# Chunks of 2, 4, 4, 3, 3, 3, 2 units with shared sigmoid phases, 8 KB output rows and 64-row combine products in a fused RG-LRU and soft-MoE kernel

## The chip, the cores and the metric

The kernel runs on one core of one Trainium2 chip. The metric is the device time of one execution in microseconds (us). A core has five engines, each with its own instruction queue in program order: TensorE (PE), VectorE (DVE), ScalarE (ACT), GpSimd (POOL) and SyncE (SP), which here only issues DMAs. Matrix products go to PSUM, everything else lives in SBUF.

## The reference

The first half is a gated linear recurrence over 4 sequences of 5056 tokens with 256 channels, the second a soft mixture of experts over the resulting 20224 tokens.

```python
log_a = 8 * sigmoid(r_gate) * log(clip(sigmoid(a_param)))
a_t = exp(log_a);  norm = sqrt(max(1 - a_t*a_t, 1e-6))
x_gated = norm * sigmoid(i_gate) * x
h = a_t[:, t]*h + x_gated[:, t];  y[:, t] = h         # for t in range(S)
logits = y @ phi                                       # 32 slots = 8 experts x 4
slot_input = softmax_over_tokens(logits).T @ y
slot_out[e] = relu(slot_input[e] @ w1[e]) @ w2[e]      # w1 256x1024, w2 1024x256
out = softmax_over_slots(logits) @ slot_out
```

The slots need every token before the experts can run, and every output row needs the experts. So all of y is computed and reduced first, and the output is written at the end. Only the logits (20224 x 32) are kept.

## The kernel before, in words

Tokens are taken in 40 quads q of 512 (four blocks of 128; the last has 256). Units p hold two quads, but the first and the last hold one: 21 units. A planner adds tasks with names, durations and buffers, and `run_fixed` emits them in the order that is written out by hand in `ORDER`, a list for each engine (line 79). Durations only settle which buffer slot a task gets. SBUF has 20 big buffers `b` of 8 KB a partition (N_B, line 52).

For each quad, D tasks load r, i and x (tokens in rows of four, 4 KB a partition). TR (line 788) transposes r to channels on partitions, SR (799) takes tanh. EX (866) takes the exponential, for two units of a chunk together where a chunk has a pair (`second`, line 762), SQ (850) squares on POOL, RT (881) takes the root. SI (812, 814) takes the input gate's sigmoid, or tanh in units marked P or E in `IV`, U (834) multiplies with x on POOL, TU (900) transposes. ST (917) and the scan SC (934) run on DVE. The tokens of a unit stand along the free dimension of A, so that y is in A after SC. TY (958) transposes y back and YC (972, 974) copies it to `yn`.

ACT holds one set of functions at a time: tanh and exp, tanh and sigmoid, or sqrt. Units are grouped in chunks (`CHUNKS`, line 23), and ACT goes through a chunk in phases: SR and EX, then SI, then RT.

For every four quads there is a group g: LG (1009) makes the logits with four quads side by side in the 128 columns of PE, LE (1022) copies them and keeps a running maximum M, LD, TE (1053) and ES (1063) make the exponentials, AC (1083) sums them times y, AE (1099) adds into `accS` with the factor DM (1070). The last four quads are split: group 9 has two, group 10 has three segments of 256 tokens. The merge (MT, MX, MR, MC, WJ, WE, W, SP, SL, DN, RD) joins the four row sets; L1 (1331) and L2 (1379) are the experts, whose weights w1 and w2 are loaded behind the gates.

SO (1398) scales the slot outputs, RS (1401) spreads them over four row sets, SH and BD (1403 to 1412) split them in a high and a low part, in a block-diagonal form for two blocks of tokens. For each group, CT (1438) transposes the logits, CM, CS, CE, RR and CN make the softmax, CH and CL split it, HP (1503) transposes, HE (1514, 1516) copies, OT (1526) multiplies two blocks at once with 128 rows by 512 columns, OE (1538, 1540) copies to an output buffer, OD (1550) writes 4 KB a partition, 512 KB in all.

## Time and profile before

| | |
|---|---|
| median of 3 runs | 300.62 us (299.88 to 300.74) |
| profiled execution | 300.04 us, span 298.3 us |
| ACT_TABLE_LOAD | 26 of 1283 ns |
| moved | 100.02 MB, of which 20.71 MB written |

A row of a list of groups reads: line, engine, operation, output<-input, count, then busy us and mean ns, then the idle time ahead of it and what ended it. A row of the timeline reads: start us, busy us, engine, line, operation, count. A row of stretches gives the busy us of each engine between two times.

### The profile page before, as it was taken

How to read it: one execution, taken by the hardware profiler on the slowest of the kernel's cores; microseconds unless marked ns; L12 is line 12 of the kernel's file. 1: busy time of each engine (PE TensorE's matmuls, PEld its weight loads, DVE VectorE, ACT ScalarE, POOL GpSimd, SP SyncE). 2: the span in 40 equal slices, each digit the busy share in tenths (PEclk: the TensorE clock that was granted, in tenths of full speed). 3: DMA queues.
4: the chain of work that ended last, by engine and by line, in shares of the span. 5: the costliest groups of instructions: out<-in, count | busy, mean ns of one | idle time of the engine just before them, and what ended most of it. 6: DMA issues, size and time to landing. Idle time of an engine off the chain costs nothing.

```text
span 298.3 us, 5854 instructions
## 1 busy us (share of the span) xinstructions
PE 259.9 (87%) x2223; PEld 198.9 (67%) x2223; DVE 232.3 (78%) x289; ACT 251.2 (84%) x271; POOL 204.5 (69%) x150
## 2 busy tenths in 40 slices
...
GB/s 229 414 409 409 402 408 410 407 408 281 322 291 208 396 415 407 274 401 116 396 392 264 174 335 365 229 385 362 358 405 351 6 78 398 404 402 404 402 409 288
DMA packets 30287, 100.02 MB, mean 335 GB/s; under 512 B 3378, under 2 KB 3380, under 8 KB 30260
## 3 DMA queue, kind: packets, MB, share of 16 engines
...
q8 instruction: 17, 0.28, 0.4%
q14 instruction: 10, 0.08, 0.1%
...
HBM read 78.94 MB, written 20.71 MB: 334 GB/s over the span
## 4 chain that ended last, share of the span: by engine, by line
PE 35%; ACT 24%; DVE 14%; DMA 11%; POOL 6%; issue 6%; SPq 0%; ACTq 0%; POOLq 0%; DVEq 0%
DVE b L934 7%; PE bank L1526 7%; DMA b<-in_i_gate_dram 6%; PE pair L788 5%; ACT b L881 4%; DVE pair L917 4%; PE pair L900 4%; POOL b L834 4%; ACT b L812 3%; DMA st<-in_moe_w_dram 3%; ACT b L799 3%; ACT b L866 3%; PE one L1526 3%; ACT L881 3%; POOL b L850 2%
## 5 line engine op out<-in xcount | busy, mean ns | idle before, releaser
L850 POOL TENSOR_TENSOR b<-b 128x1024 f32<-128x1024 f32 (+2 forms) x41 | 73.6, 1816 | 9.0 <-ACT b L866 4.7
L834 POOL TENSOR_TENSOR b<-b,b 128x1024 f32<-128x1024 f32 x32 | 75.4, 2379 | 6.0 <-ACT b L814 4.3
L917 DVE SCALAR_TENSOR_TENSOR pair<-b,pair 128x1024 f32<-128x1024 f32 (+2 forms) x42 | 47.9, 1154 | 11.9 <-ACT b L881 8.1
L900 PE MATMUL pair<-ident,b 128*128 128x128 f32 x380 | 49.4, 278 | 7.3 <-DVE b L934 3.0
L900 PEld LDWEIGHTS pair<-ident,b 128*128 128x128 f32 x380 | 42.3, 143 | 15.7 <-POOL b L834 4.7
L934 DVE TENSOR_TENSOR_SCAN b<-b,pair 128x1024 f32<-128x1024 f32 (+6 forms) x26 | 47.6, 1848 | 0.2
L788 PE MATMUL pair<-ident,st 128*128 128x128 f32 x316 | 42.1, 280 | 5.2 <-DVE b L934 2.1
L934 DVE TENSOR_TENSOR_SCAN b<-b,b,pair 128x1024 f32<-128x1024 f32 (+2 forms) x22 | 45.4, 2073 | 0.4
L788 PEld LDWEIGHTS pair<-ident,st 128*128 128x128 f32 x316 | 35.4, 143 | 12.8 <-ACT b L799 4.9
L799 ACT ACTIVATE b<-pair 128x1024 f32<-128x1024 f32 (+1 forms) x40 | 39.4, 1012 | 4.6 <-PE pair L788 4.4
L866 ACT ACTIVATE b<-b,ca 128x2048 f32<-128x2048 f32 (+3 forms) x24 | 42.7, 1795 | 0.2
L958 PE MATMUL one<-ident,b 128*128 128x128 f32 x208 | 31.6, 281 | 7.2 <-DVE yn L974 2.5
L958 PEld LDWEIGHTS one<-ident,b 128*128 128x128 f32 x208 | 22.6, 141 | 17.3 <-DVE yn L974 6.6
L1526 PE MATMUL bank<-bd,hT 128*128 128x512 f32 x118 | 31.7, 400 | 0.3 <-DVE hT L1516 0.3
L1469 POOL TENSOR_TENSOR b<-b,rs_all 128x512 f32<-128x512 f32 (+2 forms) x11 | 10.6, 960 | 29.8 <-DVE rs_all L1461 23.2
L881 ACT ACTIVATE b<-b 128x2048 f32<-128x2048 f32 (+2 forms) x17 | 29.8, 1785 | 0.1
L1514 ACT CAST hT<-bank 128x512 fp32r<-128x512 f32 x14 | 8.3, 600 | 21.4 <-PE bank L1503 20.6
L812 ACT ACTIVATE b<-b 128x2048 f32<-128x2048 f32 x14 | 26.0, 1906 | 0.1
L1526 PEld LDWEIGHTS bank<-bd,hT 128*128 128x128 f32 x118 | 21.3, 188 | 5.4 <-ACT st L1538 0.8
L1538 ACT COPY st<-bank 128x512 f32<-128x512 f32 x33 | 18.8, 603 | 6.9 <-PE bank L1526 4.5
L974 DVE COPY yn<-one 128x512 f32<-128x512 f32 x32 | 21.2, 682 | 2.2 <-PE one L958 2.1
L1009 PE MATMUL one<-b,phi_sb 128*32 128x512 f32 x152 | 21.3, 618 | 0.0
...
## 6 DMA issues: line engine op xcount, KB each, us to landing
b<-in_x_dram SPq DMA_DIRECT2D x39, 512.0 KB, 7.4
st<-in_r_gate_dram SPq DMA_DIRECT2D x38, 512.0 KB, 8.1
b<-in_i_gate_dram SPq DMA_DIRECT2D x38, 512.0 KB, 8.4
b<-in_moe_w_dram SPq DMA_DIRECT2D x28, 512.0 KB, 6.2
out_dram<-st SPq DMA_DIRECT2D x28, 512.0 KB, 4.4
out_dram<-b SPq DMA_DIRECT2D x10, 512.0 KB, 4.6
st<-in_moe_w_dram SPq DMA_DIRECT2D x4, 512.0 KB, 8.0
...
```

The source lines that it names most:

```text
L788: nc.tensor.transpose(out=o[:, m, :], in_=raw("r", q)[:, m * D + h * P : m * D + (h + 1) * P], identity=ident,)
L799: nc.scalar.activation(dst, t(rp)[:, :, :c], AF.Sigmoid if SIGR else AF.Tanh, scale=1.0 if SIGR else 0.5)
L812: nc.scalar.activation(v, v, AF.Sigmoid)
L834: eng.tensor_tensor(out=o, in0=a, in1=b, op=ALU.mult)
L850: eng.tensor_tensor(out=t(Nb[p])[:, h, :c], in0=v, in1=v, op=ALU.mult)
L866: nc.scalar.activation(v, v, AF.Exp, scale=ca[:, h : h + 1], bias=ca[:, h : h + 1])
L881: nc.scalar.activation(v, v, AF.Sqrt, bias=quarter if f != 1.0 else f, scale=-f)
L900: nc.tensor.matmul(o[:, m, :], raw(nm, q)[:, m * D + h * P : m * D + (h + 1) * P], ident, is_transpose=True, start=(nm == nms[0] and m == ...
L917: nc.vector.scalar_tensor_tensor(v, t(Nb[p])[:, h, :c], 0.5e-3 if gate_of(quads(p)[0]) == "E" else 1e-3, v, op0=ALU.max, op1=ALU.mult)
L934: nc.vector.tensor_tensor_scan(dst, dst, flat()[:, s0:s1], init, op0=ALU.mult, op1=ALU.add)
L958: nc.tensor.transpose(out=flat()[:, b * D + h * P : b * D + (h + 1) * P], in_=t(A[p])[:, h, o : o + P], identity=ident,)
L1526: nc.tensor.matmul(t(op), t(hT)[:, b * P // 2 : (b + 2) * P // 2], T["bd"][part].rearrange("p i d -> p (i d)"), start=(part == 0), stop=(p ...
```

## The change

The chunks become 2, 4, 4, 3, 3, 3, 2 units; the sigmoids of chunk 4 are taken in the sigmoid phase of chunk 3, those of chunk 6 in that of chunk 5 (`SIWITH`), and the last unit takes sigmoid in place of tanh. The order of every engine is written anew. A block of y now holds every eighth token of a unit (`tokens`), so that a partition of the output holds eight tokens in a row: OD writes 8 KB a partition, 1 MB in all, for a unit of two quads, and half of that for the first three quads. Group 0 has three quads, groups 1 to 9 four, group 10 the two blocks of the last. The combine keeps the slot outputs once, and OT takes the two blocks from the two halves of the rows, in products of 64 rows into two PSUM banks; a task covers four blocks. SO is a copy on DVE and ACT, its factor goes into R2. Some durations of the planner are changed too.

```diff
-CHUNKS = [2, 4, 4, 4, 4, 2, 1]
+CHUNKS = [2, 4, 4, 3, 3, 3, 2]
...
-IV = 'PPEEEESSSSSSSSSSSSSSP'
+IV = 'PPEEEESSSSSSSSSSSSSSS'
...
+SIWITH = {4: 3, 6: 5}
...
 ORDER = {
     "ACT": """
-        SA LN SR0 SI0 EX0.1 SR1 EX0.0 SR2 SR3 EX1.0 EX1.1 SI1 SR5 RT0.0 RT1.0 SR6 SR4 SI3 EX2.0 SR7 EX2.1 SR9 SI5 SR8 SR10 EX4.0 RT2.0 RT3.0 EX4.1
-        SR11 SI7 SR12 RT5.0 RT4.0 SR13 SI9 SR14 ES0 EX6.0 SR15 EX6.1 SR16 SR17 SR18 EX8.1 EX8.0 DM1 ES1 SI11 SI15 SI17 SI13 RT6.0 RT9.0 RT7.0 YC10.0
-        YC10.2 RT8.0 SR19 SR21 SR22 SR20 EX10.0 SR23 ES2 YC12.0 DM2 SR25 EX10.1 YC11.0 SR24 SR26 EX12.1 EX12.0 YC11.2 DM3 ES3 SI19 SI25 SI21 SI23
-        RT10.0 RT11.0 YC17.2 YC18.0 RT13.0 YC16.2 RT12.0 SR27 YC18.2 SR28 YC19.0 SR29 SR30 EX14.1 SR31 SR33 EX14.0 SR34 SR32 EX16.0 EX16.1 ES4 ES5 DM5
-        DM4 SI27 SI29 RT14.0 RT17.0 RT15.0 SI31 SR35 SI33 SR36 RT16.0 SR37 SR38 YC27.0 EX18.0 DM6 ES6 YC26.2 EX18.1 SR39 SI35 YC29.0 SI37 YC32.0
-        YC29.2 RT18.0 YC30.0 YC30.2 YC31.0 DM7 ES7 RT19.0 YC33.0 YC33.2 EX20.0 YC34.0 YC32.2 SI39 CE0 YC34.2 EX20.1 YC36.0 YC35.0 YC36.2 ES8 YC35.2
-        RT20.0 CE1 YC37.2 DM8 CE2 YC37.0 YC38.0 ES9 YC39.0 ES10 DM10 WE YC38.2 DM9 HE0.0 BD01 BD00 OE0.4 HE1.0 OE0.2 CE3 OE1.2 OE0.10 HE1.8 HE2.0
...
+        SA LN SR0 EX0.0 EX0.1 SR1 SR2 SI0 EX1.0 SR3 EX1.1 SR5 SI1 SR6 SR4 EX2.0 RT0.0 RT1.0 SR7 SI3 SR8 EX2.1 SR9 SR10 EX4.0 EX4.1 SI5 RT2.0 RT3.0
+        RT5.0 RT4.0 SI7 SR11 SR13 YC3.0 SR12 SI9 SR14 EX6.0 EX6.1 SR15 SR17 YC3.2 DM1 SR16 SR18 ES0 EX8.1 ES1 EX8.0 SI11 SI17 SI13 SI15 RT6.0 RT7.0
+        RT9.0 RT8.0 YC9.2 SR19 SR20 YC10.2 SR21 DM2 YC11.0 SR22 SR23 EX10.0 SR24 EX10.1 ES2 EX12.1 EX12.0 DM3 ES3 SI19 SI21 RT11.0 RT10.0 YC14.2
+        YC13.0 RT12.0 SI23 SR25 SI25 SI29 SR27 SI27 SR26 SR28 DM4 SR29 EX13.0 SR30 EX13.1 ES4 EX15.1 EX15.0 SR31 RT13.0 RT14.0 RT15.0 YC23.2 SR33 SR32
+        YC23.0 SR34 DM5 EX16.0 EX16.1 YC24.0 SR35 SR36 DM6 EX18.0 EX18.1 ES6 ES5 SI31 SI33 SI35 SI39 SI37 RT16.0 RT17.0 RT18.0 YC29.0 YC27.2 YC29.2
+        SR37 YC28.2 SR38 YC31.0 SR39 EX19.0 ES7 YC32.0 EX19.1 YC30.0 EX20.0 YC30.2 YC31.2 DM7 RT19.0 DM8 YC32.2 YC34.0 YC33.0 CE1 ES8 EX20.1 YC34.2
+        YC33.2 YC36.0 YC35.0 RT20.0 YC35.2 CE0 YC38.0 YC37.0 YC38.2 DM9 ES9 YC37.2 CE2 YC39.0 ES10 DM10 WE SO1 HE0.0 BD00 OE0.2 HE0.8 OE0.6 HE1.0 CE3
...
     "DVE": """
-        CA SQ0.0 U0 ST0.1 ST0.0 SC0.1 SC0.0 YC0.0 ST1.1 SC1.1 ST1.0 SC1.0 YC2.0 YC0.2 YC2.2 YC1.2 YC1.0 ST2.1 SC2.1 ST2.0 SC2.0 ST3.1 SC3.1 ST3.0
-        SC3.0 LE0 YC3.0 ST4.0 SC4.0 ST4.1 SC4.1 YC3.2 ST5.0 SC5.0 LE1 YC4.0 YC5.0 ST5.1 SC5.1 AE0 YC7.0 YC9.0 YC6.0 YC5.2 YC6.2 YC7.2 YC4.2 YC9.2
-        YC8.0 CM1 YC8.2 CS1 AE1 ST6.0 ST6.1 SC6.0 SC6.1 ST7.0 SC7.0 CM0 LE2 CS0 ST7.1 ST8.0 SC7.1 SC8.0 ST8.1 SC8.1 YC12.2 ST9.0 LE3 SC9.0 ST9.1
...
-        AE6 SC17.0 ST17.1 LE7 SC17.1 ST18.0 YC31.2 SC18.0 ST18.1 AE7 SC18.1 ST19.0 LE8 SC19.0 ST19.1 SC19.1 ST20.0 ST20.1 SC20.0 SC20.1 LE9 RR0 LE10
-        LD9 LD10 MX MR WJ AE8 AE9 W AE10 CH0 SL RD HS0 HR0 RR1 HS1 HR1 CH1 RR2 CH2 SO HE0.8 SH BD11 BD10 CM3 CS3 OE0.6 OE0.0 OE0.8 OE1.0 RR3 OE0.12
...
+        CA U0 ST0.0 ST0.1 SC0.0 SC0.1 ST1.1 SC1.1 ST1.0 SC1.0 YC0.2 YC0.0 YC1.0 YC2.0 LE0 YC1.2 YC2.2 ST2.1 ST2.0 SC2.1 SC2.0 CM0 CS0 ST3.0 SC3.0
+        ST3.1 SC3.1 ST4.0 SC4.0 ST4.1 LE1 SC4.1 ST5.0 SC5.0 ST5.1 SC5.1 YC5.0 LE2 YC4.0 AE0 YC4.2 YC6.0 YC6.2 YC5.2 YC8.0 CM1 CS1 AE1 YC7.0 YC7.2
+        YC9.0 YC10.0 YC8.2 ST6.0 ST6.1 SC6.0 SC6.1 ST7.0 CM2 SC7.0 ST7.1 CS2 SC7.1 ST8.0 YC12.0 SC8.0 LE3 ST8.1 YC11.2 SC8.1 ST9.0 AE2 SC9.0 ST9.1
...
+        ST17.0 SC17.0 ST17.1 SC17.1 ST18.0 SC18.0 LE8 ST18.1 AE7 SC18.1 ST19.0 ST19.1 SC19.0 SC19.1 ST20.0 YC36.2 AE8 LE9 SC20.0 ST20.1 SC20.1 LE10
+        RR0 MX MR WJ W AE9 AE10 SL RR2 CH0 RD HS0 HR0 RR1 HS1 CH2 HR1 CH1 SO SH BD10 CM3 OE0.0 OE0.4 CS3 OE0.10 OE1.0 OE1.2 RR3 CM4 CS4 CH3 OE2.0 RR4
...
     "SP": """
...
-        Dx38 Dx39 w23 w24 w10 w27 w21 w14 w12 w16 w20 w11 w15 w17 w22 w26 OD0.1 OD0.0 OD1.0 OD0.2 OD0.3 OD1.1 OD2.0 OD2.1 OD2.3 OD1.3 OD2.2 OD1.2
...
+        w22 w23 w20 Dx39 w24 w15 w12 w21 w13 w26 w10 w17 w11 w14 w16 w25 w27 OD0.0 OD0.1 OD0.2 OD1.0 OD1.2 OD2.0 OD2.2 OD3.0 OD3.2 OD4.2 OD4.0 OD5.2
...
-    groups = [[(q, 0, QT) for q in range(g, g + J)] for g in range(0, NQ - J, J)]
-    rest = list(range(len(groups) * J, NQ))
-    groups.append([(q, 0, QT) for q in rest[:2]])
-    half = QT // 2
-    tail = []
-    for q in rest[2:]:
-        tail += [(q, o, half) for o in range(0, qlen(q), half)]
-    assert len(rest) == J and len(tail) <= J and all(qlen(q) % half == 0 for q in rest)
-    groups.append(tail)
+    groups = [[(q, 0, QT) for q in range(J - 1)]]
+    groups += [[(q, 0, QT) for q in range(g, g + J)] for g in range(J - 1, NQ - 1, J)]
+    groups.append([(NQ - 1, o, P) for o in range(0, qlen(NQ - 1), P)])
     NGR = len(groups)
+
+    def tokens(q, b0=0, nb=J):
+
+        p, i = unit[q]
+
+        def view(h):
+            v = t(A[p])[:, h, : plen(p)].rearrange("q (c m) -> q m c", c=P)
+            k = i * J + b0
+            return v[:, k, :] if nb == 1 else v[:, k : k + nb, :]
+
...
                 for b in range(nb):
-                    o = i * QT + (b0 + b) * P
                     for h in range(H):
                         nc.tensor.transpose(
                             out=flat()[:, b * D + h * P : b * D + (h + 1) * P],
-                            in_=t(A[p])[:, h, o : o + P],
+                            in_=tokens(q, b0 + b, 1)(h),
                             identity=ident,
                         )
 
...
             def e_lg(h=h):
                 for j, (q, o, _) in enumerate(segs):
-                    o += unit[q][1] * QT
                     nc.tensor.matmul(
                         t(lp)[32 * j : 32 * j + NS, :L], phi_sb[:, h, :],
-                        t(A[unit[q][0]])[:, h, o : o + L], start=(h == 0), stop=(h == H - 1),
+                        tokens(q, o // P, L // P)(h), start=(h == 0), stop=(h == H - 1),
...
-        gs = sorted(cq[k], key=lambda q: gate_of(q) == "S")
+        gs = sorted([q for k2 in range(NC) for q in cq[k2] if SIWITH.get(k2, k2) == k], key=lambda q: gate_of(q) == "S")
         gs = [q for q in gs if (not SIM or gate_of(q) == "S") and not late_i(q)]
...
             nc.vector.tensor_scalar(small["rd"], t(sp)[:, P : P + 1], 1e-9, None, op0=ALU.add)
             nc.vector.reciprocal(small["rd"], small["rd"])
-
+            nc.vector.tensor_scalar(small["R2"], R.rearrange("p j s -> p (j s)"), small["rd"], None, op0=ALU.mult)
...
 
     def e_bz():
 
-        T["bd"] = [sb.tile([P, 2, D], F32R, name=f"bd{i}", tag="eS", bufs=2) for i in range(2)]
+        T["bd"] = [sb.tile([P, 2, D], F32R, name="bd0", tag="eS", bufs=2)]
         T["hT"] = [sb.tile([P, QT], F32R, name=f"hT{i}", tag="lD", bufs=2) for i in range(2)]
-        for b in T["bd"]:
-            nc.gpsimd.memset(b.bitcast(F32), 0.0)
-
-    t_bz = add("POOL", "BZ", 0.8, deps=[*AE.values()], prio=-60, alloc=[bdb], emit=e_bz)
-    a = add("DVE", "SO", 0.35, deps=[l2_prev, t_rd], prio=-60, uses=[so], alloc=[soSb], emit=lambda: nc.vector.tensor_scalar(
-        t(soSb), t(so)[:, :D], small["rd"], None, op0=ALU.mult))
+
+    t_bz = add("POOL", "BZ", 0.01, deps=[*AE.values()], prio=-60, alloc=[bdb], emit=e_bz)
+    def e_so(i):
+        c = slice(i * half, (i + 1) * half)
+        if i:
+            nc.scalar.copy(out=t(soSb)[:, c], in_=t(so)[:, c])
+        else:
+            nc.vector.tensor_copy(out=t(soSb)[:, c], in_=t(so)[:, c])
+
+    t_so = add("DVE", "SO", 0.2, deps=[l2_prev], prio=-60, uses=[so], alloc=[soSb], emit=lambda: e_so(0))
+    t_so = [t_so, add("ACT", "SO1", 0.17, deps=[l2_prev], prio=-60, uses=[so, soSb], emit=lambda: e_so(1))]
     sr = Buf("one", "sr")
-    a = add("PE", "RS", 0.44, deps=[a], prio=-60, alloc=[sr], uses=[soSb], shape="M", emit=lambda: nc.tensor.matmul(
-        t(sr)[:, :D], R.rearrange("p j s -> p (j s)"), t(soSb), start=True, stop=True))
+    a = add("PE", "RS", 0.44, deps=[*t_so, t_rd], prio=-60, alloc=[sr], uses=[soSb], shape="M", emit=lambda: nc.tensor.matmul(
+        t(sr)[:, :D], small["R2"], t(soSb), start=True, stop=True))
...
-    def e_b(part, i):
-        r = slice(i * P // 2, (i + 1) * P // 2)
-        dst = T["bd"][part][r, i, :]
+    def e_b(part):
+        dst = T["bd"][0][:, part, :]
         if part:
-            nc.vector.tensor_tensor(out=dst, in0=t(sr)[r, :D], in1=t(soHb)[r], op=ALU.subtract)
+            nc.vector.tensor_tensor(out=dst, in0=t(sr)[:, :D], in1=t(soHb), op=ALU.subtract)
         else:
-            nc.scalar.copy(out=dst, in_=t(soHb)[r])
-
-    t_bd = [add("DVE" if part else "ACT", f"BD{part}{i}", 0.35, deps=[a, t_bz], prio=-60, uses=[soHb, bdb] + ([sr] if part else []),
-                emit=lambda part=part, i=i: e_b(part, i)) for part in range(2) for i in range(2)]
+            nc.scalar.copy(out=dst, in_=t(soHb))
+
+    t_bd = [add("DVE" if part else "ACT", f"BD{part}0", 0.35 if part else 0.28, deps=[a, t_bz], prio=-60,
+                uses=[soHb, bdb] + ([sr] if part else []), emit=lambda part=part: e_b(part)) for part in range(2)]
 
...
-            v = lS(g)[:rows, :L].rearrange("q (p n) -> q n p", n=nb)
+            v = lS(g)[:rows, :L].rearrange("q (n p) -> q n p", n=nb)
...
-            for b in range(0, aw, 2):
+            for b in range(0, aw, J):
+                nk = min(J, aw - b) // 2
                 j, b0 = (a0 + b) // nb, (a0 + b) % nb
-                op = Buf("one", f"op{g}.{a0 + b}")
-
-                def e_ot(b=b, op=op, hT=hT):
-                    for part in range(2):
-                        nc.tensor.matmul(
-                            t(op), t(hT)[:, b * P // 2 : (b + 2) * P // 2],
-                            T["bd"][part].rearrange("p i d -> p (i d)"),
-                            start=(part == 0), stop=(part == 1),
-                        )
-
...
+                ops = [Buf("one", f"op{g}.{a0 + b}.{x}") for x in range(2)]
+
+                def e_ot(b=b, ops=ops, hT=hT, nk=nk):
+                    for k in range(nk):
+                        for part in range(2):
+                            for x in range(2):
+                                r = slice(x * P // 2, (x + 1) * P // 2)
+                                c = (b // 2 + k) * P
+                                nc.tensor.matmul(
+                                    t(ops[x])[:, k * D : (k + 1) * D], t(hT)[r, c : c + P], T["bd"][0][r, part, :],
+                                    start=(part == 0), stop=(part == 1),
+                                )
+
+                k = add("PE", f"OT{g}.{a0 + b}", 0.23 * nk, deps=[he, *t_bd], prio=pr + b * 0.1,
+                        emit=e_ot, alloc=ops, uses=[hT, bdb], shape="F")
+
+                for x in range(2):
+
+                    def e_oe(op=ops[x], og=ogs[j], w=wide[j], nk=nk, x=x):
+                        dst = t(og)[:, w : w + 2 * nk * D].rearrange("p (k x d) -> p x k d", x=2, d=D)[:, x]
+                        v = t(op)[:, : nk * D].rearrange("p (k d) -> p k d", d=D)
...
+
+                    x_ = add(("DVE", "ACT"), f"OE{g}.{a0 + b + 2 * x}", 0.07 + 0.265 * nk, deps=[k], prio=pr + b * 0.1,
...
         for j, (q, o, _) in enumerate(segs):
-
-            def e_od(q=q, o=o, L=L, nb=nb, og=ogs[j]):
-                a0 = q * QT + o
-                nc.sync.dma_start(
-                    out=out[a0 : a0 + L, :].rearrange("(p n) d -> p (n d)", n=nb), in_=t(og)[:, : nb * D])
-
-            add("SP", f"OD{g}.{j}", 1.30 * nb / J, deps=done[j], prio=100 + 8 * i + 4 + j, emit=e_od, uses=[ogs[j]], kind="out")
+            if o:
+                continue
+            two = len(quads(unit[q][0])) == 2
+            if two and g > 0 and unit[q][1]:
+                continue
+
+            def e_od(q=q, og=ogs[j], g=g):
+                p, i = unit[q]
+                t0 = UNITS[p][0] * QT
+                v = out[t0 : t0 + plen(p), :].rearrange("(m n) d -> m (n d)", n=plen(p) // P)
+                s = t(og)[:, : plen(p) // P * D]
+                if g == 0 and len(quads(p)) == 2:
+                    v, s = v[:, i * J * D : (i + 1) * J * D], s[:, i * J * D : (i + 1) * J * D]
+                nc.sync.dma_start(out=v, in_=s)
+
+            of = [j] if g == 0 else [j, j + 1] if two or L < QT else [j]
+            add("SP", f"OD{g}.{j}", 1.28 * (2 * P if L < QT else QT * len(of)) / QT, deps=[x for a in of for x in done.get(a, [])],
+                prio=100 + 8 * i + 4 + j, emit=e_od, uses=[ogs[j]], kind="out")
...
```

180 lines of the change are left out of this document (98 added, 82 removed).

## The prediction

> **What bounds the kernel now.** I read the page first, then the busy times of stretches cut where VectorE (DVE) takes up the next chunk.
>
> ```profile
> span 298.3 us, 5854 instructions
> PE 259.9 (87%) x2223; PEld 198.9 (67%) x2223; DVE 232.3 (78%) x289; ACT 251.2 (84%) x271; POOL 204.5 (69%) x150
> GB/s 229 414 409 409 402 408 410 407 408 281 322 291 208 396 415 407 274 401 116 396 392 264 174 335 365 229 385 362 358 405 351 6 78 398 404 402 404 402 409 288
> ```
> ```profile
> core 0: us, PE busy (x) PEld busy (x) DVE busy (x) ACT busy (x) POOL busy (x), PEclk, DMA share, GB/s
> 43.06:87.38 44.32, 40.52 (x366) 31.50 (x365) 39.96 (x40) 43.98 (x32) 39.58 (x22) 1.00 0.95 370
> 87.38:213.96 126.58, 109.54 (x969) 77.45 (x967) 123.86 (x115) 123.83 (x116) 107.37 (x59) 0.99 0.84 318
> 213.96:223.62 9.66, 8.27 (x75) 5.63 (x76) 6.85 (x22) 4.16 (x12) 2.90 (x4) 1.00 0.98 381
> 223.62:243.61 19.99, 19.99 (x294) 13.64 (x295) 9.31 (x21) 1.98 (x4) 5.88 (x5) 1.00 0.36 135
> 243.61:298.30 54.69, 45.84 (x237) 36.94 (x235) 35.02 (x73) 38.92 (x76) 16.35 (x16) 0.97 0.96 380
> ```
> The share of the whole span makes PE look like the bound. By stretch it is not. From 87.38 to 213.96 us, the end of the last scan, ACT is idle for 2.75 us of 126.58 and DVE for 2.72: two engines bound this stretch together. From 43.06 to 87.38 ACT has 0.34 us idle and DVE 4.36. Then come the merge of the groups (213.96 to 223.62) and the experts, where PE is busy for all of its 19.99 us. From 243.61 on, the output is written at 398 to 409 GB/s in the six full slices, close to the best rate of the loads (415), so the DMA engines bound it; PE, ACT and DVE have 9 to 20 us to spare there.
>
> **ACT: fewer function tables.** The lists of both orders are compared from the end of EX1.1 to RT20.0. A table load is needed where the function changes set; tanh stands with exp and with sigmoid.
>
> ```profile
> L881 ACT ACT_TABLE_LOAD x10 | 12.8, 1283 | 0.2
> L799 ACT ACT_TABLE_LOAD x5 | 6.4, 1283 | 0.1
> L812 ACT ACT_TABLE_LOAD x5 | 6.4, 1283 | 0.1
> L866 ACT ACT_TABLE_LOAD x2 | 2.6, 1283 | 0.0
> L972 ACT COPY yn<-one 128x512 f32<-128x512 f32 x20 | 11.3, 580 | 0.0
> ```
> ```profile
> 7.59 1.06 ACT L814 ACTIVATE st<-st 128x1024 f32<-128x1024 f32 x1 [0.28 <-DMA st<-in_i_gate_dram]
> ...
> 10.08 1.02 ACT L799 ACTIVATE b<-pair 128x1024 f32<-128x1024 f32 x1 [0.72 <-PE pair L788]
> ...
> 13.51 2.37 ACT L866 ACTIVATE b<-b,ca 128x1024 f32<-128x1024 f32 x2
> 15.78 1.91 ACT L814 ACTIVATE b<-b 128x2048 f32<-128x2048 f32 x1
> 18.62 1.28 ACT L881 ACT_TABLE_LOAD   x1
> 19.91 2.86 ACT L881 ACTIVATE b<-b 128x1024 f32<-128x1024 f32 x2
> ...
> 41.02 3.91 ACT L881 ACTIVATE b<-b,quarter 128x2048 f32<-128x2048 f32 x2
> ...
> 70.74 4.08 ACT L866 ACTIVATE b<-b,ca 128x2048 f32<-128x2048 f32 x2
> 74.73 0.28 ACT L1070 ACTIVATE dm<-M 128x1 f32<-128x1 f32 x1
> ```
> A load takes 1.29 us from its start to the next function (18.62 to 19.91). By the rule of sets the old order needs 25 loads up to RT20.0 and the new one 21: two fall away because chunk 1 takes its four roots in one batch, the others because the sigmoids of chunks 4 and 6 ride with those of 3 and 5. That is 4 x 1.29 = -5.2 us. Chunks of three leave one unit without a partner, so four double exponentials become eight single ones: a double one takes 2.00 (70.74 to 74.73 for two), a single one 1.135 (13.51 to 15.78 for two), 8 x 1.135 - 4 x 2.00 = +1.1. One copy YC fewer is -0.5 and a small exponential about +0.2. The sum is **-4.4 us of ACT work**. The Trainium skill (ScalarE: Activation LUTs, section What ACT_TABLE_LOAD costs) adds a drain of about 1.38 us to each load; by it four loads would be worth 10.6. The trace disagrees: the next function starts 1.29 us after the load does, so the sum goes by the row.
>
> **DVE: hardly less work.** Its list from ST2 to SC20.1 has the same scans, products and copies as before, and one AE more (0.48 us, row 221.90). So it ends earlier only if it starts earlier or waits less.
>
> ```profile
> 43.06 1.23 DVE L917 SCALAR_TENSOR_TENSOR pair<-b,pair 128x1024 f32<-128x1024 f32 x1 [4.31 <-ACT b L881]
> ...
> 212.58 1.38 DVE L934 TENSOR_TENSOR_SCAN b<-b,b,pair 128x256 f32<-128x256 f32 x2
> ...
> 214.99 0.67 DVE L1459 TENSOR_REDUCE rs_all<-b 128x16 f32<-128x512 f32 x1
> ...
> 216.37 0.48 DVE L1022 TENSOR_SCALAR_CACHE_REDUCE b<-bank,M 96x256 f32<-96x256 f32 x1
> ...
> 221.90 0.48 DVE L1099 SCALAR_TENSOR_TENSOR accS<-accS,dm,bank 96x257 f32<-96x257 f32 x1
> ```
> ```profile
> 87.38 2.36 DVE L917 SCALAR_TENSOR_TENSOR pair<-b,pair 128x1024 f32<-128x1024 f32 x2 [1.39 <-ACT b L881]
> ```
> Both marks at which DVE starts a chunk wait for ACT's roots (43.06, 87.38). In the new list one double exponential more (EX4.1, 2.0 us) stands ahead of RT2.0, against up to 1.0 us that the earlier issue of the first r tiles can win (the waits of 0.72 and 0.28 in the rows above): ST2 starts at about 44.5. RT6.0 has two loads fewer ahead of it (-2.6) but two YC copies more (+1.0): it ends 1.6 us earlier, at about 85.7. DVE needs 39.96 us of work between them, so the 4.36 us that it idles there now shrink to 1.2, and it reaches ST6 between 85.7 and 44.5 + 44.3 = 88.8; I take 86.5, nearer to the first because copies fill the wait. Behind it DVE has its 126.58 us with 2.72 idle, so the last scan ends at 86.5 + 126.6 = 213, **1 us earlier**, and most of ACT's 4.4 us turn into idle time of ACT. Were DVE never idle after ST6, it would be 4 us. POOL keeps its products (11 to 15% idle in these rows); the sixteen small copies of R only move.
>
> **The merge.** Now 8.4 us lie between the last scan (213.96) and the end of the last AE (222.38). LE10 starts 2.4 us after the scan, because LE9 and a first RR0 (row 214.99) run on DVE ahead of it; in the new list LE9 and AE8 come ahead of SC20.1 and RR0 comes behind LE10.
>
> ```profile
> 215.10 1.53 PE L958 MATMUL bank<-ident,b 128*128 128x128 f32 x12
> ...
> 219.03 2.80 PE L1083 MATMUL bank<-yn,eS 128*32 128x257 f32 x28
> ```
> ```profile
> 122.28 1.88 PE one L1083 x32
> ```
> PE then does the last transposes and 28 products with yn in 2.80 us. The new last groups need 8 transposes, not these 12 and 8 more behind them (about 1.0 us by row 215.10), 32 products with four groups side by side (1.9, row 122.28) and 4 more (0.3). With LG10 (0.5), the small transposes and hand-overs (1.2) and the AE (0.5) that makes about 5.4 us: **-3 us**. If only LE10's delay goes it is -1.6; the experts' weights can take 1 us back, for w10, w11, w14 and w16 now come among the last seven of the sixteen, and the loads end only about 231 (slice 31 shows 6 GB/s).
>
> **From the experts to the first output.**
>
> ```profile
> 238.86 0.48 DVE L1398 TENSOR_SCALAR hs<-one,rd 128x256 f32<-128x256 f32 x1 [0.60 <-PE one L1379]
> ...
> 240.74 0.86 DVE L1410 TENSOR_TENSOR bd<-one,hs 64x256 fp32r<-64x256 f32 x2
> ```
> ```profile
> 243.61 3.72 SPq L1550 DMA_DIRECT2D out_dram<-st  x4
> ```
> The 0.48 us of SO are halved between DVE and ACT (about -0.2; the extra R2 product stands under the expert products), two BD become one (-0.43), and the first 512 KB need one product of four blocks instead of two of two (0 to -0.45): **-0.9 us**.
>
> **The output.**
>
> ```profile
> 261.49 2.72 PE bank L1526 x12
> ...
> 259.24 0.87 PE bank L1503 x8
> ...
> 255.39 0.48 PE one L1438 x4
> ```
> A product of 128 rows and 512 columns takes 0.227 us, two for two blocks. The new form streams the same 1024 columns for two blocks in four products of 64 rows, and loads four sets of weights instead of two. No row shows two row halves at work; side by side it is 0.23 us for two blocks, one after the other 0.45, and with uncovered weight loads at most about 0.64 (a 128-column transpose with its load takes 0.11, row 259.24; a 256-column product about 0.05 more; times four). Four blocks are 512 KB, 1.28 us at 405 GB/s. PE has 0.22 for HP and 0.12 for CT besides, so up to 0.47 us for two blocks it stays under the DMA engines' 1.28; I take 0 either way. Rows of 8 KB move the same bytes; 4 KB loads reach 414 and 4 KB stores 409, which bounds the effect at about half a us either way; I take 0. A first 1 MB transfer waits for eight blocks, and three 512 KB ones ahead of it cover that.
>
> **Strided reads.** Tokens of a unit now lie eight apart on a partition, so LG's moving operand and TY's weights step by 32 bytes, and CT's, which stepped by 16, is contiguous. Four CT take 0.48 us, 0.12 each, against 0.11 for the contiguous HP above, so for 300 TY the stride costs at most 3 us of a PE with 17 us idle in its stretch. A strided moving operand has no row; between nothing and twice its 1.02 us for LG, I take nothing, nearer to CT.
>
> ```profile
> 172.12 1.02 PE one L1009 x8
> ```
>
> **The sum.** -1 (DVE's start), -3 (merge), -0.9 (first output), 0 (output): -4.9 us from the profiled execution's 300.04, which is a span of 298.3 and 1.7 around it; that execution lies 0.6 under the median of 300.62. 300.04 - 4.9 = **295.1 us**, said as 295. Its own range is 292.5 to 298.
>
> **Rivals.** (B) ACT decides: the whole 4.4 us reach the end, since DVE's waits vanish too. For it: DVE waited for ACT's roots at both marks. Against it: DVE is 98% busy after 87.38. 300.04 - 4.4 - 3 - 0.9 = 291.7.
>
> (C) The loads don't shorten anything. Taking sigmoids of two chunks together keeps the i and x tiles of three more units in the 20 buffers, and SP, one queue in order, holds up the r tiles behind them.
>
> ```profile
> b<-in_i_gate_dram SPq DMA_DIRECT2D x38, 512.0 KB, 8.4
> ```
> One tile that is issued only when ACT is ready for it costs up to 8.4 us, half of that if it is under way: 295.1 + 4.2 = 299.3, no measurable change; two of them, or a whole one, 303. Against it: the DMA engines have 16% of the time free after 87.38.
>
> (D) The slower side: LG's strided operand. At twice its price the 18 tasks LG1 to LG9 cost 18 x 1.02 = 18 us of PE, which has 3.8 + 17.0 = 20.8 idle there. If half of that idle time is bound to waits, growth starts at 0.6 us for a task, the gain is gone at 0.85, and at 1.02 it is 295.1 + 8 = 303. Against it: CT's 16-byte step costs next to nothing. The Trainium skill (SBUF — State Buffer, the note on cachelines in the section Door 1: The DMA port swizzle) states that reads which move to a new 16-byte line each time pay a penalty, which speaks for D; no run so far shows it for a moving operand.
>
> (E) The 64-row products at 0.64: PE needs 1.62 us for four blocks against 1.28, times 39.5: 295.1 + 13 = 308.
>
> **Chances.** Forecast 0.50, B 0.23, C 0.15, D 0.08, E 0.04. A difference of 0.3%, 0.9 us, is about what a measurement can tell from none. Faster by more: the forecast, B and 0.09 of C, 0.82; within: 0.03 of C and 0.03 of D and E where their prices are small, 0.06; slower: 0.03 of C and 0.09 of D and E, 0.12. The range of 290 to 301 takes in B and the cheap half of C and leaves out D and E.
>
> **What would show it.** 22 table loads in place of 26. The last scan's end about 213 (B: under 210.5; C: 214 or later). The last AE 5 to 6 us behind it. Out rows at about 405 GB/s in every full slice; L1526's successor at half its PE time or the same makes no difference to the end. LG tasks of eight records at 1.0 us (D: 1.9 or more). The forecast is wrong if the last scan moves by over 3 us, or the output slices fall under 390 GB/s.

## The result: 6% slower, and the profile after

| | before | changed |
|---|---|---|
| median | 300.53 us (299.88 to 300.74, 4 runs) | 318.66 us (316.66 to 319.17, 4 runs) |
| ratio | | 1.0595, 95% interval 1.0546 to 1.0643 |
| profiled execution | 300.04 us, span 298.3 | 318.87 us, span 317.1 |

The prediction was 295 us, with a range of 290 to 301. Three views of the changed kernel show most of what happened. First the page: the span, the busy times, and in 40 slices the clock that PE was granted and the rate of the DMA engines.

```profile
span 317.1 us, 6051 instructions
PE 272.5 (86%) x2345; PEld 198.1 (62%) x2345; DVE 235.0 (74%) x288; ACT 246.9 (78%) x270; POOL 205.3 (65%) x152
PEclk9998998699998899799999999999995999999895
GB/s 228 417 409 404 409 362 394 274 339 367 317 242 265 401 190 361 417 144 222 379 278 415 207 378 89 246 396 399 319 326 257 148 2 361 412 383 355 414 395 301
```

ACT has the 4.3 us less work that the prediction gave it (251.2 before, 246.9 now), DVE hardly changes, and PE has 12.6 us more, although the products of the combine got cheaper. The groups of instructions say which (the row of LG before first, then the changed kernel):

```profile
L1009 PE MATMUL one<-b,phi_sb 128*32 128x512 f32 x152 | 21.3, 618 | 0.0
```
```profile
L1019 PE MATMUL one<-b,phi_sb 128*32 128x512 f32 (+1 forms) x164 | 40.7, 1053 | 0.4 <-ACT eS L1077 0.4
L969 PEld LDWEIGHTS one<-ident,b 128*128 128x128 f32 x204 | 27.4, 195 | 12.9 <-DVE yn L985 3.2 <-issue 3.1 <-ACT yn L983 2.6
L1559 PE MATMUL bank<-bd,hT 64*128 64x256 f32 x246 | 25.9, 302 | 2.8 <-ACT hT L1542 1.9 <-ACT bd L1432 0.4 <-DVE hT L1544 0.4
L1559 PE MATMUL one<-bd,hT 64*128 64x256 f32 x70 | 11.6, 313 | 1.3 <-ACT hT L1542 1.0 <-DVE hT L1544 0.3
```

LG, with its operand stepping by 32 bytes, keeps PE busy for 40.7 us in place of 21.3: rival D. Without the eight short products the mean is 1092 ns. The weight loads of TY take 195 ns, where those of the kernel before took 141. The combine (L1559) takes 37.5 us, where it took 44.6.

The stretches, cut at the same events as before: DVE's first ST of unit 2, of unit 6, the end of the last scan, the first expert product, the first output copy, the end.

```profile
core 0: us, PE busy (x) PEld busy (x) DVE busy (x) ACT busy (x) POOL busy (x), PEclk, DMA share, GB/s
0.00:47.43 47.43, 39.30 (x285) 33.18 (x286) 16.86 (x19) 42.22 (x34) 34.63 (x36) 0.96 0.96 371
47.43:96.06 48.63, 43.51 (x335) 32.29 (x333) 40.21 (x42) 40.59 (x32) 36.20 (x19) 0.93 0.85 324
96.06:231.17 135.11, 123.59 (x986) 85.24 (x984) 124.40 (x117) 122.03 (x121) 108.35 (x74) 0.97 0.79 298
231.17:240.62 9.45, 6.25 (x62) 4.07 (x59) 6.26 (x15) 2.78 (x9) 3.41 (x4) 0.85 0.98 361
240.62:260.97 20.35, 19.87 (x284) 11.41 (x286) 7.05 (x21) 1.25 (x3) 5.72 (x5) 0.90 0.29 108
260.97:317.10 56.13, 40.01 (x406) 31.92 (x402) 40.20 (x79) 38.07 (x76) 16.99 (x16) 0.90 0.90 370
```

The kernel before has 43.06, 44.32, 126.58 and 9.66 us for the first four, and with the same cut for the last two:

```profile
223.62:242.84 19.22, 19.22 (x291) 12.98 (x292) 8.63 (x20) 1.39 (x3) 5.88 (x5) 1.00 0.37 140
242.84:298.30 55.46, 46.61 (x240) 37.60 (x238) 35.70 (x75) 39.51 (x77) 16.35 (x16) 0.97 0.94 374
```

That is +4.4, +4.3, +8.5, -0.2, +1.1 and +0.7 us. In the long stretch PE is now busy for 123.59 of 135.11 us, and DVE, which was never idle for long, waits 10.7. PE has become the bound there.

### The profile page after: what moved, and what is told of

It reads as the page before. It is cut to its first block, busy times and chain, and to the rows that moved or that the text cites. A ratio compares the mean times of both kernels' runs of the same rounds, so it can differ in the third digit from the quotient of the medians.

```text
span 317.1 us, 6051 instructions
## 1 busy us (share of the span) xinstructions
PE 272.5 (86%) x2345; PEld 198.1 (62%) x2345; DVE 235.0 (74%) x288; ACT 246.9 (78%) x270; POOL 205.3 (65%) x152
## 4 chain that ended last, share of the span: by engine, by line
PE 59%; DVE 19%; ACT 6%; issue 5%; POOL 4%; DMA 4%; SPq 1%; DVEq 0%; ACTq 0%; POOLq 0%
PE one L1019 12%; PE pair L912 11%; DVE b L946 7%; PE one L969 6%; PE pair L800 6%; DVE pair L929 5%; PE bank L1559 4%; PE one L1097 4%; PE pair L969 3%; DMA st<-in_i_gate_dram 3%; ACT b L811 2%; PE bank L1394 2%; DVE yn L985 2%; PE bank L1531 2%; PE one L1346 2%
## 5 line engine op out<-in xcount | busy, mean ns | idle before, releaser
L846 POOL TENSOR_TENSOR b<-b,b 128x1024 f32<-128x1024 f32 x38 | 89.4, 2379 | 7.4 <-ACT b L826 5.6
L912 PE MATMUL pair<-ident,b 128*128 128x128 f32 x380 | 52.7, 290 | 5.7 <-DVE b L946 2.8
L912 PEld LDWEIGHTS pair<-ident,b 128*128 128x128 f32 x380 | 45.9, 150 | 12.5 <-POOL b L846 4.7
L946 DVE TENSOR_TENSOR_SCAN b<-b,b,pair 128x1024 f32<-128x1024 f32 (+3 forms) x24 | 47.0, 1971 | 0.2
L946 DVE TENSOR_TENSOR_SCAN b<-b,pair 128x1024 f32<-128x1024 f32 (+5 forms) x24 | 45.9, 1927 | 0.2
L1019 PE MATMUL one<-b,phi_sb 128*32 128x512 f32 (+1 forms) x164 | 40.7, 1053 | 0.4 <-ACT eS L1077 0.4
L969 PEld LDWEIGHTS one<-ident,b 128*128 128x128 f32 x204 | 27.4, 195 | 12.9 <-DVE yn L985 3.2
L1559 PE MATMUL bank<-bd,hT 64*128 64x256 f32 x246 | 25.9, 302 | 2.8 <-ACT hT L1542 1.9
L1573 ACT COPY b<-bank 128x512 f32<-128x512 f32 x40 | 22.4, 609 | 6.1 <-PE bank L1559 3.2
L1559 PEld LDWEIGHTS bank<-bd,hT 64*128 64x128 f32 x246 | 20.8, 191 | 6.2 <-ACT hT L1542 2.9
L969 PEld LDWEIGHTS pair<-ident,b 128*128 128x128 f32 x104 | 13.6, 193 | 13.9 <-issue 9.4
```

The source lines that it names most:

```text
L846: eng.tensor_tensor(out=o, in0=a, in1=b, op=ALU.mult)
L912: nc.tensor.matmul(o[:, m, :], raw(nm, q)[:, m * D + h * P : m * D + (h + 1) * P], ident, is_transpose=True, start=(nm == nms[0] and m == ...
L946: nc.vector.tensor_tensor_scan(dst, dst, flat()[:, s0:s1], init, op0=ALU.mult, op1=ALU.add)
L969: nc.tensor.transpose(out=flat()[:, b * D + h * P : b * D + (h + 1) * P], in_=tokens(q, b0 + b, 1)(h), identity=ident,)
L1019: nc.tensor.matmul(t(lp)[32 * j : 32 * j + NS, :L], phi_sb[:, h, :], tokens(q, o // P, L // P)(h), start=(h == 0), stop=(h == H - 1),)
L1559: nc.tensor.matmul(t(ops[x])[:, k * D : (k + 1) * D], t(hT)[r, c : c + P], T["bd"][0][r, part, :], start=(part == 0), stop=(part == 1),)
```

## The experiments

Theory 1 said that LG's strided operand costs the time. Rival 2 blamed the new order and chunks, rival 3 TY's strided weights. The first four kernels tell these apart.

**1. LG over neighbouring tokens.**

```diff
-                        tokens(q, o // P, L // P)(h), start=(h == 0), stop=(h == H - 1),
+                        flat_tokens(q, o // P, L // P)(h), start=(h == 0), stop=(h == H - 1),
```

`flat_tokens` is A from `i * QT + b0 * P` on, `nb * P` columns in a row.

> The changed kernel, but LG reads 512 neighbouring tokens of its quad in place of every eighth token; so the logits belong to other tokens than the rows of y that they are paired with, and the output is not the reference's; the amount of work is the same. Theory 1 (LG's strided moving operand costs twice its time and holds up PE where others wait for it): an LG product goes from 1092 ns back to about 620, a task of eight from 2.05 to about 1.0 us, PE loses 18 us of work, and the time falls from 318.7 to 300 to 306. Rival 2 (the new order and chunks themselves cost the time): PE loses the same work, but the time stays at 313 or more. Rival 3 (TY's strided weights): 313 or more as well.

Measured: 302.58 us, ratio to before 1.0052 (1.0022 to 1.0083). LG takes 21.0 us again:

```profile
L1025 PE MATMUL one<-b,phi_sb 128*32 128x512 f32 (+1 forms) x164 | 21.0, 584 | 0.4 <-ACT eS L1083 0.4
```

16.1 of the 18.1 us are gone with one line, where rivals 2 and 3 gave 313 us or more. Theory 1 holds.

**2. TY over neighbouring tokens.**

```diff
-                            in_=tokens(q, b0 + b, 1)(h),
+                            in_=flat_tokens(q, b0 + b, 1)(h),
```

> The changed kernel, but TY transposes 128 neighbouring tokens in place of every eighth token, so that y is paired with the logits of other tokens and the output is not the reference's; the amount of work is the same. Rival 3 (TY's strided weights): a weight load goes from 195 to about 141 ns, and the time falls by 5 us or more. Theory 1 and rival 2: the loads shorten, the time falls by less than 3 us.

Measured: 313.33 us, 1.0416 (1.0385 to 1.0446), 5.3 us under the changed kernel. By this run rival 3 is right about its 5 us, and theory 1, which gave less than 3, is not; the next one shows that TY isn't the main cause.

**3. Both over neighbouring tokens.** The two edits together.

> The changed kernel with LG and TY both reading neighbouring tokens; the output rows hold other tokens than their weights, the work is the same. Theory 1: what is left of the change is the chunks, the merge and the output of the prediction, at 295 to 301. Rival 2: 312 or more.

Measured: 301.32 us, 1.0010 (0.9984 to 1.0037). Beside a contiguous LG, TY's stride is worth 302.58 - 301.32 = 1.3 us; beside a strided LG it was 5.3, since PE was the bound then. The two together cost 17.3 us. What remains of the change, freed of its strides, makes no measurable difference: 301.3, just above the 295 to 301 that theory 1 gave. So 6 us of the prediction were still missing. The stretches of this kernel say where:

```profile
0.00:45.51 45.51, 38.91 (x292) 34.87 (x293) 16.95 (x19) 40.70 (x34) 33.36 (x35) 0.96 0.98 379
45.51:90.27 44.76, 39.07 (x333) 30.89 (x332) 39.69 (x41) 40.30 (x31) 36.83 (x20) 0.92 0.94 357
90.27:215.07 124.80, 108.77 (x982) 79.69 (x979) 123.52 (x116) 122.47 (x121) 108.90 (x74) 0.99 0.84 319
215.07:225.20 10.13, 7.08 (x61) 3.84 (x59) 6.26 (x16) 2.71 (x8) 3.42 (x4) 0.83 0.99 394
```

The last scan ends at 215.07, not 213, and the merge takes longer than before. Experiments 7 and 10 look into both.

**4. The kernel before, with LG strided and nothing else.**

```diff
-                        t(A[unit[q][0]])[:, h, o : o + L], start=(h == 0), stop=(h == H - 1),
+                        lgv(q, o, L, h), start=(h == 0), stop=(h == H - 1),
```

`lgv` gives, for groups 1 to 8, columns stepping by eight floats.

> The kernel before, with LG of groups 1 to 8 reading every eighth token (in units of two quads), and nothing else changed; the logits are paired with other tokens, so the output is not the reference's. Theory 1: these products take about 1090 ns for 618, 16 us more of PE, and the time grows by 8 to 16 us. Rival 2 and 3: at most 3 us.

Measured: 310.33 us, 1.0316 (1.0284 to 1.0349).

```profile
L1016 PE MATMUL one<-b,phi_sb 128*32 128x512 f32 x152 | 36.3, 1014 | 0.0
```

15.0 us more on PE cost 9.4 us of time here, where rivals 2 and 3 gave at most 3. By rival D's rule (10.4 us of PE's idle time take the growth first) it would have been 4.6. The changed kernel turned 19.7 us into 16.1 (experiment 1), because its PE had more to do and waited at other places.

**5. The price by step.** Groups 1 to 8 of the kernel before read A each in another way (`rearrange` of the unit's 1024 columns or the quad's 512), and TY too. Two of the eight ways are shown.

```diff
-                        t(A[unit[q][0]])[:, h, o : o + L], start=(h == 0), stop=(h == H - 1),
+                        lgv(q, o, L, h), start=(h == 0), stop=(h == H - 1),
...
+            if g == 1:
+                return a.rearrange("q (c m) -> q m c", m=2)[:, i, :]
...
+            if g == 4:
+                return a.rearrange("q (c m) -> q c m", m=8)[:, :, i * J : (i + 1) * J]
```

> The kernel before, with another way of reading A in every group, for the price of one product (LG) or one weight load (TY) alone; tokens are mixed up, so the output is not the reference's. LG: group 1 reads every second float (steps of 8 bytes), group 2 every fourth (16 bytes), group 3 every eighth (32 bytes), group 6 every sixteenth (64 bytes), group 4 runs of four floats every 32 bytes, group 5 runs of two every 16 bytes, group 8 runs of eight every 64 bytes, group 7 neighbours but writes them to PSUM in steps of 512 bytes. TY: units 4 to 7 step by 8 bytes, 8 to 11 by 16, 12 to 15 by 32. Theory A (a price per 16-byte line that is touched): steps of 8 bytes and runs of two cost 1.0 to 1.3 times the 618 ns, 16 bytes and above twice, runs of four and of eight once. Theory B (any step other than one element costs twice): groups 1, 2, 3 and 6 all at 1090 ns, runs of two, four and eight in between. Theory C (a price that grows with the step): 32 bytes twice, 16 bytes less, 64 bytes more than twice. TY by theory A or C: 141 ns at 8 bytes, up to 195 at 32.

One run took 303.38 us; its time is not the point, the prices are. The products of one group each (minimum/median/maximum ns, then first and last start): group 1, 2, 3, 4, 5, 6, 7, 8.

```profile
L1038 PE MATMUL one<-b,phi_sb x16: 609/624/637, 63.2 to 70.4; 128*32 128x512 f32 x16
L1038 PE MATMUL one<-b,phi_sb x16: 1064/1078/1087, 92.6 to 97.1; 128*32 128x512 f32 x16
L1038 PE MATMUL one<-b,phi_sb x16: 1082/1090/1097, 109.0 to 113.4; 128*32 128x512 f32 x16
L1038 PE MATMUL one<-b,phi_sb x16: 592/592/617, 135.1 to 136.8; 128*32 128x512 f32 x16
L1038 PE MATMUL one<-b,phi_sb x16: 610/624/638, 148.9 to 151.5; 128*32 128x512 f32 x16
L1038 PE MATMUL one<-b,phi_sb x16: 1024/1077/1136, 174.4 to 178.4; 128*32 128x512 f32 x16
L1038 PE MATMUL one<-b,phi_sb x16: 592/592/617, 193.9 to 195.2; 128*32 128x512 f32 x16
L1038 PE MATMUL one<-b,phi_sb x16: 592/593/617, 206.2 to 207.9; 128*32 128x512 f32 x16
```

Steps of 8 bytes, and runs of two floats in every 16 bytes, cost nothing to speak of (624). From 16 bytes on a record takes 1.75 times as long (1078, 1090, 1077) and a task of eight twice (2.0 us for 1.0), and a longer step adds nothing. Runs of four and eight floats cost 592, and so does a write to PSUM in steps of 512 bytes. That is theory A: two floats out of each 16 bytes are enough, one is not. The Trainium skill (SBUF — State Buffer, the note on cachelines in the section Door 1: The DMA port swizzle) says that a 16-byte line needs two or more hits for the full rate; the run agrees to the step.

The granted clock of PE was 1.00 in seven of these eight stretches. In group 2 it was 0.50 for the first eight products (92.64 to 94.65 us) and 1.00 for the last eight (96.21 to 98.20 us):

```profile
L1038 PE MATMUL one<-b,phi_sb x8: 1078/1082/1087, 92.6 to 93.6; 128*32 128x512 f32 x8
L1038 PE MATMUL one<-b,phi_sb x8: 1064/1072/1079, 96.2 to 97.1; 128*32 128x512 f32 x8
```

So the price of the step is there at the full clock, and half the clock adds nothing to it. A product over neighbouring tokens does slow down: six of experiment 7, at a clock of 0.50 (38.39 to 40.32 us), took 1062 ns each.

Weight loads follow another rule. The loads of TY in four stretches: without a step, then in units that step by 8, by 16 and by 32 bytes:

```profile
L966 PEld LDWEIGHTS one<-ident,b x24: 138/141/144, 24.0 to 54.7; 128*128 128x128 f32 x24
...
L966 PEld LDWEIGHTS one<-ident,b x20: 194/209/220, 102.9 to 118.5; 128*128 128x128 f32 x20
...
L966 PEld LDWEIGHTS one<-ident,b x8: 195/209/213, 139.4 to 145.1; 128*128 128x128 f32 x8
...
L966 PEld LDWEIGHTS one<-ident,b x20: 185/191/205, 180.2 to 189.4; 128*128 128x128 f32 x20
```

Any step costs some 50 to 70 ns, 8 bytes as much as 32, so this part of theory A was wrong.

**6. Runs of four.** LG reads the four neighbours of each eight as a run; the logits then stand in the order of time, and TE and CT step over them.

```diff
+            return v[:, :, k : k + nb]
...
-                        t(lp)[32 * j : 32 * j + NS, :L], phi_sb[:, h, :],
-                        tokens(q, o // P, L // P)(h), start=(h == 0), stop=(h == H - 1),
+                        t(lp)[32 * j : 32 * j + NS, :L].rearrange("q (c m) -> q c m", c=P), phi_sb[:, h, :],
+                        runs(q, o // P, L // P)(h), start=(h == 0), stop=(h == H - 1),
...
-                    out=t(ep)[:, b * rows : (b + 1) * rows], in_=t(lD)[:rows, b * P : (b + 1) * P],
+                    out=t(ep)[:, b * rows : (b + 1) * rows], in_=t(lD)[:rows, :L].rearrange("q (c m) -> q m c", c=P)[:, b, :],
...
-            v = lS(g)[:rows, :L].rearrange("q (n p) -> q n p", n=nb)
+            v = lS(g)[:rows, :L].rearrange("q (p n) -> q n p", n=nb)
```

> The changed kernel with the whole computation, but LG reads the four neighbouring tokens of each eight as a run (16 bytes out of every 32) in the order of time, and the transposes of the logits (TE, CT) step by 16 bytes over what it wrote. Theory A: LG at about 620 ns, and the time comes near that with LG over neighbouring tokens, 302 to 304. Theory B or C: LG stays at 900 or more, and the time at 312 or more.

Measured: 305.19 us (302.68 to 305.81), 1.0126 (1.0079 to 1.0173). LG takes 21.0 us, as in experiment 1. The 8 KB rows of the output and a cheap LG go together. The time lies 1.2 us over the range that was expected and 2.6 over experiment 1, which has TY's stride as well. New here is that TE and CT load weights in steps of 16 bytes; no run separates what that costs from the spread of the four executions.

**7. Another order in the merge.** In experiment 3 two small operations of DVE take 1.75 and 1.36 us (they take 0.17 and 0.21 elsewhere), and each ends within 0.1 us of an operation of POOL. DVE's rows, then POOL's and PE's:

```profile
216.53 1.75 DVE L1486 TENSOR_SCALAR rs_all<-rs_all 128x12 f32<-128x12 f32 x1
...
218.70 1.36 DVE L1290 COPY mrep<-mmax 1x128 f32<-1x128 f32 x1
```
```profile
216.44 1.80 POOL L1332 MEMSET b<- 128x2048 f32 x1
...
219.45 0.53 POOL L1273 MEMSET yn<- 128x512 f32 x1
```
```profile
220.11 0.58 PE L1292 MATMUL bank<-ones,mrep 1*128 1x1 f32 x2 [2.09 <-DVE mrep L1290]
220.62 2.78 PE L1103 MATMUL bank<-yn,eS 128*32 128x257 f32 x20
```

```diff
     "DVE": """
-        RR0 MX MR WJ W AE9 AE10 SL RR2
+        MX MR WJ W AE9 AE10 SL RR0 RR2
     "POOL": """
-        LD9 LD10 HZ CN0 SZ CN1
+        LD9 LD10 SZ CN0 HZ CN1
```

> The third experiment's kernel (LG and TY over neighbouring tokens, the output rows hold other tokens than their weights), with another order in the merge: on VectorE the first RR0 comes behind SL, on GpSimd the 1.8 us fill HZ comes behind CN0 and the small fill SZ ahead. Theory 4 (two small VectorE operations wait for GpSimd's fill and product, which is where the 3 us of the merge went): the add L1486 takes 0.2 us in place of 1.75 and the copy L1290 0.2 to 0.5 in place of 1.36, PE's wait of 2.1 us shrinks to under 1, the granted clock behind it stays at 1.0, and the time falls by 2.5 to 4.5 us, to 297 to 299. Rival 5 (these two operations are slow for a reason of their own): they stay slow, and the time changes by less than 1 us.

Measured: 298.78 us, 0.9929 (0.9900 to 0.9959), 2.5 us under experiment 3. The profiled execution took 300.36 us, where the ten lie between 296.95 and 301.07; its last scan ends 1.7 us later than that of experiment 3.

```profile
219.13 0.22 DVE L1290 COPY mrep<-mmax 1x128 f32<-1x128 f32 x1
...
221.10 1.07 DVE L1119 SCALAR_TENSOR_TENSOR accS<-accS,dm,bank 128x257 f32<-128x257 f32 x2 [0.32 <-PE bank L1103]
...
224.89 2.18 DVE L1486 TENSOR_SCALAR rs_all<-rs_all 128x16 f32<-128x16 f32 x1
```
```profile
225.24 1.81 POOL L1332 MEMSET b<- 128x2048 f32 x1
```

The copy is quick, PE's 20 products behind it take 1.50 us in place of 2.78, the last scan ends at 216.77 and the last AE at 222.17: 5.40 us, the figure of the prediction. The fill has found another victim: an add that ends at 227.07, where the fill ends at 227.05. The place matters less there.

**8. Experiments 6 and 7 together.**

> The sixth and the seventh experiment together, with the whole computation. Theory A and theory 4 both right: 298 to 301, at or below the kernel before. Theory A wrong: 308 or more. Theory 4 wrong: 302 to 304.

Measured: 300.56 us, 0.9983 (0.9956 to 1.0010), level with the kernel before and in the range that was given for both theories right. The new order is worth 4.6 us here, beside experiment 6, and was worth 2.5 beside experiment 3; the four executions of experiment 6 spread over 3.1 us, so this difference may be chance.

**9. The fill behind W.** The planner's task HZ gets W as a dependency, and its place ahead of CN0.

```diff
-    t_hz = add("POOL", "HZ", 1.6, deps=[ST[(NP - 1, H - 1)]], prio=500, alloc=[hz],
+    t_hz = add("POOL", "HZ", 1.6, deps=[ST[(NP - 1, H - 1)], t_w], prio=500, alloc=[hz],
```

> The eighth experiment's kernel (whole computation), with the fill HZ made to wait for the task W, so that it runs on GpSimd while VectorE reads PSUM only, and CN0 behind it. Theory 4 (VectorE's copies and adds wait for GpSimd's fill): the add of 2.18 us that the seventh experiment still had (L1486, a second place where it met HZ) falls to 0.2, PE's wait of 0.58 us for the first hidden rows goes, and the time falls by 0.3 to 1.5 us against the eighth. Rival 5: an operation of nearly 2 us is there again, wherever HZ is put, without a collision, and the time stays.

Measured: 300.84 us, 0.9993 (0.9970 to 1.0016). The edit did not do what it was meant to: nothing in the data ties the fill to W, so it ran right behind SZ, ahead of W, and met the copy again:

```profile
219.01 1.35 DVE L1295 COPY mrep<-mmax 1x128 f32<-1x128 f32 x1
```
```profile
218.47 1.81 POOL L1337 MEMSET b<- 128x2048 f32 x1
```

The copy ends at 220.36, the fill at 220.28; the add that suffered in experiment 7 takes 0.43. The time did not fall either. In three orders the long one is whichever copy or add meets the fill. Rival 5 falls.

**10. PE kept busy.** In the kernels with the new order PE stands still for 3 to 4 us from 46 to 49 us on, since TR needs a `pair` buffer that a scan frees. The clock is halved after that:

```profile
50.00:52.00 2.00, 0.59 (x3) 0.60 (x4) 2.00 (x2) 1.98 (x2) 2.00 (x2) 0.71 1.03 418
52.00:54.00 2.00, 1.73 (x9) 1.33 (x8) 2.00 (x2) 1.99 (x3) 1.37 (x2) 0.50 0.94 377
```

(Stretches of experiment 9; the clock stands behind the five engines.)

```diff
-            for b in range(nb):
+            for b in list(range(nb)) * (8 if g == 0 else 1):
                 nc.tensor.transpose(out=o[:, b], in_=v[:, b, :], identity=ident[:rows, :rows])
```

> The ninth experiment's kernel, with the transposes CT0 made eight times over the same output, so that PE works from 46 to 49 us in place of standing still for 3.8 us ahead of the first TR of the next chunk; the result is the same. Theory 6 (PE's clock is halved some 2 us after PE has stood still, for about 7 us, and that holds up the TR tasks that ACT waits for): the granted clock between 48 and 56 us stays at 1.0, the TR at 50 takes 1.0 us in place of 1.97, DVE's wait of 3 us for TU at 56 falls below 2, the scan of unit 6 starts 1 to 3 us earlier, and the time falls by 1 to 2.5 us. Rival 7 (the clock falls for another reason, or the time lies elsewhere): the clock falls as before, or the time changes by less than 0.5 us.

Measured, beside experiment 9 on the same chip: 299.80 us against 300.84. The ratio to the kernel before is 0.9959 (0.9932 to 0.9986), where experiment 9 has 0.9993 (0.9970 to 1.0016). The TR behind the gap in experiment 9, and in this one:

```profile
51.41 1.97 PE L811 MATMUL pair<-ident,st 128*128 128x128 f32 x8 [3.12 <-DVE b L957]
```
```profile
47.10 3.98 PE L1469 MATMUL one<-ident,b 96*128 96x96 f32 x32
50.92 1.04 PE L811 MATMUL pair<-ident,st 128*128 128x128 f32 x8
```

The clock stays at 1.00 from 48 to 58 us, TR takes half the time, and the stretch from the first ST of unit 2 to that of unit 6 falls from 44.95 (46.73 to 91.68) to 43.07 us (46.17 to 89.24). DVE's wait for TU falls from 3.40 to 1.51 us. What theory 6 says of the clock holds. In the time it is 1 us, the low end of what it gave, and the two intervals overlap a little, so the time alone would not show it.

**11. The fill between LD9 and LD10.**

```diff
-        LD9 LD10 SZ HZ CN0 CN1
+        LD9 HZ LD10 SZ CN0 CN1
```

The dependency of experiment 9 is taken out again; the repeated CT0 of experiment 10 stays.

> The tenth experiment's kernel (whole computation), with the fill HZ between LD9 and LD10, where VectorE has a scan and the last reduction to do and no copy but two of 0.15 us. Theory 4: the copy L1295 takes 0.2 us in place of 1.35, the adds behind SL 0.2 to 0.4, PE's wait of 0.8 us ahead of the small products goes, and the time falls by 1 to 1.5 us against the tenth, to 298 to 299.3; a collision with the two copies of M costs 0.5 us of that. Rival 5: one operation of over 1 us is there again, and the time stays at 299.5 to 301.

Measured: 298.59 us, 0.9936 (0.9912 to 0.9960), in the range of theory 4. The interval overlaps that of experiment 10, so what the fill's place alone is worth is read from the rows. The copy takes 0.22 us, the two copies of M 0.31 together as ever, and the last AE ends 5.45 us behind the last scan (215.65 to 221.10). This kernel computes all that the changed one does, and it beats both: 2 us under the kernel before, 20 under the change as it was made.

## Why the prediction was wrong, point by point

**The step that failed first is "Strided reads", the 0 for LG's operand.** The prediction had no row for a strided moving operand and set its price by the nearest one, CT, a weight load with a step of 16 bytes. That row could not carry it: a weight load pays 50 to 70 ns at any step and hides most of that, a moving operand pays double from 16 bytes on (experiment 5). Rival D named the mechanism and the price of 1.02 us more for a task (1.0 to 2.0 measured), with a chance of 0.08, although a stated rule spoke for it. Its sum was too small as well: it let half of PE's idle time, 10.4 us, take the growth, so that 8 of 18 us arrived. In the kernel before 5.6 us were taken (9.4 of 15.0 arrived, experiment 4). In the changed kernel 3.6 were, and 16.1 of 19.7 us arrived, for PE, at 123.59 of 135.11 us, had become the engine that the others wait for.

**TY's weights.** "At most 3 us" was right by itself (1.3, experiment 3 against 1), wrong in company (5.3, experiment 2).

**ACT and the tables.** Right. The changed kernel has the 22 table loads of the prediction. ACT loses 5.7 us of work in experiment 3 (251.24 to 245.51) and 4.3 in the changed kernel, for the 4.4 of the sum. As the prediction said, little of it reaches the end.

**DVE's start** (ST2 at 44.5, ST6 at 86.5, last scan 213). Experiment 3, without the strides, has 45.51, 90.27 and 215.07. The long stretch was right, even 1.8 us better (124.80 for 126.6). The step that failed is "copies fill the wait", by which DVE's idle time between the two marks would shrink to 1.2 us (the 86.5 that was taken leaves 2.0): it stayed at 5.1 (44.76 less 39.69). PE stands still for 4 us in the new order and then works at half its clock, so that TU and TR come late to DVE and ACT. Experiment 10 takes 1.9 us of this away in the kernel of experiment 9; the rest stays open. The clock may hold more of it: its mean is 0.942 to 0.974 in every execution of the new order and 0.982 to 0.991 in those of the kernel before on the same chips, and of the ten executions of experiment 7 the shortest (296.95 us) has 0.974, the longest (301.07) 0.947.

**The merge, -3 us.** The 5.4 us between the last scan and the last AE were worked out rightly and are there in experiments 7 and 11 (5.40 and 5.45). In experiment 3 they were 8.86 (215.07 to 223.93), since the order set POOL's fills beside an add and a copy of DVE. The prediction counted each operation at its own length and left out what runs beside it. PE's wait of 2 us for the copy is followed by half the clock. In experiment 3 this falls on the 20 products with yn (2.78 us for 1.50). In the changed kernel it comes later (the last row is a stretch, with the clock behind the engines), and the experts' first 64 products take 5.65 us, where experiment 7 has 3.66:

```profile
236.21 0.38 PE L1286 MATMUL bank<-ones,mrep 1*128 1x1 f32 x2 [2.04 <-DVE mrep L1284]
...
240.62 5.65 PE L1346 MATMUL one<-b,yn 128*32 128x256 f32 x64 [0.39 <-DVE yn L1308]
```
```profile
238.00:244.00 6.00, 4.85 (x40) 2.93 (x42) 2.59 (x10) 0.00 (x0) 0.00 (x0) 0.50 0.53 209
```

**From the experts to the first output, -0.9.** Right: from the last AE to the first OE experiment 3 has 19.62 us, the kernel before 20.46.

**The output, 0.** Right within 0.4 us (55.85 for 55.46 in experiment 3). Two row halves do work side by side: in the changed kernel, from 273.55 to 274.26 us, two products of 64 rows start together every 0.12 us, which is 0.23 us for two blocks, the lowest of the three prices that the prediction gave. So rival E falls. The sign that the prediction set, 405 GB/s in every full slice, was too strict: the full slices of the changed kernel go from 355 to 414, some above the best of before (409) and some with gaps. By its limit of 390 the output would have counted as wrong, and its stretch grew by 0.4 to 0.7 us.

**The sum of what was left out**, experiment 3 against 295.1: start and middle +2.1, merge +3.5, output +0.4, experts +0.1, together 6.1 of the 6.2 us of its profiled execution (301.26). The 17.3 us for the strides are the rest, as the difference of two measured times. Rival B (last scan under 210.5) shows in none of experiments 3 and 7 to 11. Rival C's sign (214 or later) does show, 215.07 in experiment 3, but not its cause: from 46 us to the last scan no engine waits for a load there. Before 46 us PE waits 1.1 us for r tiles, where the kernel before has 0.2, so up to 1 us of ST2's lateness can be C's.
